# Splitting the second expert's up-projection in the last pair and moving its last part behind three output tiles

## The chip, the cores and the metric

One core of a Trainium2 chip runs the whole program. The metric is device time in microseconds of one execution. A core has TensorE (PE, with its weight loads shown as PEld), VectorE (DVE), ScalarE (ACT), GpSimd (POOL) and SyncE (SP); SP, ACT and POOL also issue DMAs. PSUM is where TensorE leaves its sums, and an engine must copy them out of it.

## The reference

Three stages follow each other. Attention of 2 batches, 8 heads and 576 positions with a learned distance bias gives x of 1152 tokens by 512. A dense layer with the gate h·sigmoid(h) and 2048 inner columns follows. Then comes a mixture of 8 experts, of which each token takes its best two:

```
for e in range(E):
    for k in range(2):
        mask = top2[:, k] == e
        h = np.maximum(x[mask] @ w1[e], 0.0)
        out[mask] += top2_w[mask, k, None] * (h @ w2[e])
```

w1[e] is 512 by 1024 and w2[e] 1024 by 512. Every token's row of the output is a sum over two experts.

## The kernel before

Products are made in two 16-bit halves (high and low), three matmuls to each: high·high, high·low, low·high. The experts are worked in four pairs, g = 0 to 3, by `experts(g)` (line 967). Each expert has 320 slots (`CAP`), and a token routed to it holds one. The gathered, transposed token rows of a pair lie in one tile `xg` of 640 columns: columns 0 to 319 are slots 0 to 319 of the first expert; of the second, columns 320 to 383 are slots 256 to 319, columns 384 to 511 slots 128 to 255, and columns 512 to 639 slots 0 to 127.

`up(k, c0, n)` (line 971) projects n columns from c0 of expert k up. It has eight groups, one for each 128 inner columns. A group is 12 matmuls (lines 979 to 981) into a PSUM tile `ph`, of which there are three; ACT takes the ReLU's high half out of it (line 985) and DVE the low half (line 986), into a tile `ht` of that expert and group.

`down(k, c0, col)` (line 989) makes an output tile for 128 slots: 24 matmuls of 512 columns (lines 995 to 997) over the eight `ht` into a PSUM tile `po`, of which there are two. `down_last()` (line 1001) makes the shared output tile: slots 256 to 319 of both experts, 64 rows each, in 48 matmuls with 64 weight columns (line 1010). `emit_out` (line 961) scales `po` on ACT into one of four SBUF tiles `ot` (line 964), and POOL adds the rows to the output in HBM with an indirect, accumulating DMA (line 958), here called a scatter. The shared tile has two scatters of 64 rows, the others have one of 128. All scatters add to the same output tensor, and each waits on POOL until the one before it has landed.

Each engine executes its own instructions in order. The order is made when the program is built: in general the order in which the code is written, but where a simulated timeline finds an instruction waiting, a later one that is ready may be put ahead. The last pair runs alone (line 1048); conversions and gathers of the earlier pairs are interleaved with the experts' work, but none are left here. After it comes a block for overfull experts (line 1053), which is not entered with these inputs, and the end of the program.

Of the kernel before, what the change touches and what calls it, by code (L numbers as in the profile page):

```python
# [23 lines left out]
CAP = 320  # L24
# [84 lines left out]
def body(ctx, tc, nc, A):  # L109
# [37 lines left out]
    def gen(name="gen"):  # L147
        return ps.tile([128, 512], F32, name=name, tag="gen", bufs=3)
# [484 lines left out]
    def chain(*gs):  # L633
        for g in gs:
            yield from g
# [325 lines left out]
    def emit_out(g, po, p0, n, col, icol):  # L961
        idx, ws = IDX[g]
        ot = m2o.tile([128, DM], F32, name="ot", tag="ot", bufs=4)
        SC.activation(ot[:n], po[p0:p0 + n, :DM], AF.Copy, scale=ws[p0:p0 + n, col:col + 1])  # L964
        scatter(idx[:n, 1, icol:icol + 1], ot[:n])

    def experts(g):
        xg = XG[g]
        hts = {}

        def up(k, c0, n):

            a_h, a_l = EW[2 * g + k, 0]
            for f in range(8):
                ph = gen("ph")[:, :n]
                for j in range(4):
                    cs = slice(1024 * j + 128 * f, 1024 * j + 128 * f + 128)
                    xh, xl = xg[:, j, c0:c0 + n], xg[:, 4 + j, c0:c0 + n]
                    mm(ph, a_h[:, cs], xh, start=(j == 0), stop=False)  # L979
                    mm(ph, a_h[:, cs], xl, start=False, stop=False)  # L980
                    mm(ph, a_l[:, cs], xh, start=False, stop=(j == 3))  # L981
                if (k, f) not in hts:
                    hts[k, f] = m2.tile([128, 2, CAP], F16, name="ht", tag="ht", bufs=20)
                ht = hts[k, f][:, :, c0 - CAP * k:c0 - CAP * k + n]
                SC.activation(ht[:, 0], ph, AF.Relu)  # L985
                V.scalar_tensor_tensor(ht[:, 1], ph, 0.0, ht[:, 0], op0=OP.max, op1=OP.subtract)  # L986
                yield

        def down(k, c0, col):
            b_h, b_l = EW[2 * g + k, 1]  # L990
            po = ps.tile([128, S], F32, name="po", tag="pq", bufs=2)
            for f in range(8):
                cs = slice(512 * f, 512 * f + 512)
                lh, ll = hts[k, f][:, 0, c0:c0 + 128], hts[k, f][:, 1, c0:c0 + 128]
                mm(po[:, :DM], lh, b_h[:, cs], start=(f == 0), stop=False)  # L995
                mm(po[:, :DM], lh, b_l[:, cs], start=False, stop=False)  # L996
                mm(po[:, :DM], ll, b_h[:, cs], start=False, stop=(f == 7))  # L997
            emit_out(g, po, 0, 128, col, col)
            yield

        def down_last():
            po = ps.tile([128, S], F32, name="po", tag="pq", bufs=2)
            for f in range(8):
                for x in range(3):
                    for kk in range(2):
                        bh, bl = EW[2 * g + kk, 1]
                        cs = slice(512 * f, 512 * f + 512)
                        c0 = 256 if kk == 0 else 0
                        lt = hts[kk, f][:, 1 if x == 2 else 0, c0:c0 + 64]
                        mm(po[64 * kk:64 * kk + 64, :DM], lt, (bl if x == 1 else bh)[:, cs],  # L1010
                           start=(f == 0 and x == 0), stop=(f == 7 and x == 2))
            emit_out(g, po, 0, 64, 4, 4)
            emit_out(g, po, 64, 64, 4, 5)
            yield

        if g == 0:
            yield from chain(up(0, 0, 128), up(1, 512, 128), down(0, 0, 0), down(1, 192, 1), up(0, 128, 192), up(1, 320, 192))
        else:
            yield from chain(up(0, 0, CAP), up(1, CAP, CAP))
        yield from down_last()  # L1020
        if g > 0:
            yield from chain(down(0, 0, 0), down(1, 192, 1))
        yield from chain(down(0, 128, 2), down(1, 64, 3))

    first = experts(0)
    for _ in range(X0):
        next(first)
# [16 lines left out]
    for g in range(4):  # L1044
        if g < 3:
            run((first if g == 0 else experts(g), 21), (conv_pair(g + 1), 16), (gather_pair(g + 1), 2))
        else:
            run((experts(g), 1))
# [85 lines left out]
```

## Time and profile before

| what | us |
|---|---|
| median of 3 runs | 755.66 |
| lowest and highest | 752.59, 762.42 |
| profiled execution, its time | 758.37 |
| profiled execution, its span | 756.6 |

The profile is of one execution. Its span goes from the first to the last recorded instruction; 1.77 us of its time lie around that. Times in rows are from the span's start. A matmul's own duration in a row includes its way through the array, so what a stream of them costs is read from the distance between starts.

### The profile page before, as it was taken

The numbers are of one execution on the slowest core, as the hardware profiler recorded it, in microseconds if no ns is written. First come the engines' busy times: TensorE is split into PE (matmuls) and PEld (weight loads), VectorE is DVE, ScalarE is ACT, GpSimd is POOL, SyncE is SP. The second block draws the span as 40 slices with busy tenths as digits, with TensorE's granted clock in tenths as the row PEclk, the third lists the DMA queues.
The fourth block names the chain that finished last, engine by engine and source line by source line (L and its number), as shares of the span: only waits on it lengthen the run. The fifth ranks groups of instructions, "written<-read, shape, count | busy, mean of one in ns | idle before, by whom it ended". The sixth has DMA issues, their size and how long they took to land.

```text
span 756.6 us, 16562 instructions
## 1 busy us (share of the span) xinstructions
PE 606.9 (80%) x6371; PEld 402.6 (53%) x6371; DVE 502.3 (66%) x1093; ACT 377.9 (50%) x805; POOL 366.5 (48%) x366
## 2 busy tenths in 40 slices
PE   0565666578587878997999889979889899999992
PEld 0462344456344666565765664757665554655640
DVE  2999999999999699556952755656657642740200
ACT  2666467668644577345732644761355543541210
POOL 2686677687967687436761552303405114103022
PEclk9875557599788998998999999999999999999996
DMA  4547788778876699887996967764999959903123
GB/s 113 135 140 243 158 161 179 183 210 186 159 179 182 161 174 199 145 172 116 159 237 124 183 129 220 192 225 110 238 240 246 308 182 230 299 4 42 17 25 43
DMA packets 203143, 125.77 MB, mean 166 GB/s; under 512 B 153076, under 2 KB 175732, under 8 KB 203060
## 3 DMA queue, kind: packets, MB, share of 16 engines
q1 hardware_dynamic: 170868, 90.39, 52.2%
q10 hardware_dynamic: 27648, 24.32, 11.0%
q0 software_dynamic: 4544, 9.97, 7.1%
q8 instruction: 51, 0.84, 0.4%
q14 instruction: 32, 0.26, 0.1%
HBM read 74.83 MB, written 18.22 MB: 123 GB/s over the span
## 4 chain that ended last, share of the span: by engine, by line
PE 29%; DVE 29%; DMA 18%; issue 11%; ACT 4%; POOL 4%; SPq 3%; ACTq 1%; another core or an unknown queue 1%; DVEq 0%; POOLq 0%
DMA stg<-in_e 6%; DVE mk L337 4%; PE ph L979 3%; DVE z L431 3%; DMA pt<-pr 3%; PE ph L981 3%; DVE pr L442 3%; PE ph L980 3%; DVE tt L504 3%; DVE tt L505 3%; PE po L1010 3%; DVE tt L500 2%; PE po L996 2%; PE po L995 2%; PE po L997 2%
## 5 line engine op out<-in xcount | busy, mean ns | idle before, releaser
L117 POOL TENSOR_TENSOR pr<-z,pr 128x512 f16<-128x512 f32 x72 | 94.6, 1321 | 23.3 <-ACT pr L438 14.7
L553 PE MATMUL ph<-xT,wb 128*128 128x256 f16 (+1 forms) x320 | 84.9, 275 | 11.5 <-DVE th L558 7.1
L345 PE MATMUL pb<-rhs_h,mk 128*128 128x64 f16 (+1 forms) x720 | 66.4, 210 | 26.4 <-ACT ta L361 11.6
L337 DVE TENSOR_TENSOR mk<-io,tau 128x1024 f16<-128x1024 f16 (+1 forms) x90 | 85.8, 959 | 0.7 <-PE pb L346 0.7
L117 POOL TENSOR_TENSOR gt<-th,gt 128x256 f16<-128x256 f32 (+1 forms) x80 | 56.0, 704 | 60.6 <-ACT gt L562 58.1
L117 POOL TENSOR_TENSOR g<-ta 128x256 f32<-128x256 f32 (+1 forms) x72 | 63.6, 884 | 44.3 <-ACT ta L361 37.4
L554 PE MATMUL ph<-xT,wb 128*128 128x256 f16 (+1 forms) x320 | 84.8, 275 | 0.0
L555 PE MATMUL ph<-xT,wb 128*128 128x256 f16 (+1 forms) x320 | 84.8, 275 | 0.0
L958 POOL DMA_INDIRECT out<-ot,idx x18 | 27.6, 1536 | 114.5 <-ACT ot L964 52.5
L388 PE MATMUL pq<-km,qt 128*128 128x512 f16 (+2 forms) x160 | 51.7, 437 | 28.9 <-DVE st L431 28.4
L436 ACT ACTIVATE z<-z,st 128x576 f32<-128x576 f32 x72 | 55.3, 769 | 34.9 <-DVE st L435 34.4
L986 DVE SCALAR_TENSOR_TENSOR ht<-ph,ht 128x320 f16<-128x320 f32 (+2 forms) x80 | 32.8, 420 | 54.3 <-ACT ht L985 53.8
L345 PEld LDWEIGHTS <-mk 128*128 128x128 f16 (+1 forms) x720 | 57.8, 111 | 19.3 <-issue 7.7
L346 PEld LDWEIGHTS <-mk 128*128 128x128 f16 (+1 forms) x720 | 56.9, 112 | 20.1 <-issue 19.2
L346 PE MATMUL pb<-rhs_l,mk 128*128 128x64 f16 (+1 forms) x720 | 65.9, 209 | 0.0
L924 DVE SCALAR_TENSOR_TENSOR wb<-stg,wb 128x1024 f16<-128x1024 f32 (+1 forms) x48 | 48.3, 1042 | 23.6 <-ACT wb L923 20.2
L923 ACT ACTIVATE wb<-stg 128x1024 f16<-128x1024 f32 (+1 forms) x48 | 41.8, 908 | 33.5 <-DMA stg<-in_e 29.9
L576 PE MATMUL py<-wb,gt 128*128 128x512 f16 x144 | 56.0, 391 | 1.5 <-DVE st L431 1.3
L577 PE MATMUL py<-wb,gt 128*128 128x512 f16 x144 | 56.1, 389 | 1.1 <-POOL wb L511 1.1
L578 PE MATMUL py<-wb,gt 128*128 128x512 f16 x144 | 55.8, 388 | 0.0
L985 ACT ACTIVATE ht<-ph 128x320 f16<-128x320 f32 (+2 forms) x80 | 29.2, 378 | 50.0 <-PE ph L981 49.8
L511 POOL TENSOR_TENSOR wb<-tt,wb 128x512 f16<-128x512 f32 x32 | 43.7, 1366 | 17.3 <-ACT wb L510 17.1
(198 smaller groups left out, 1794.0 us busy)
## 6 DMA issues: line engine op xcount, KB each, us to landing
stg<-in_e SPq DMA_DIRECT2D x64, 512.0 KB
raw<-in_w_in ACTq DMA_DIRECT2D x16, 512.0 KB
raw<-in_w_out ACTq DMA_DIRECT2D x16, 512.0 KB
bt<-eb SPq DMA_DIRECT2D x24, 288.0 KB
eb<-g SPq DMA_DIRECT2D x12, 512.0 KB
yrows<-yh SPq DMA_DIRECT2D x9, 256.0 KB
out<-zero SPq DMA_DIRECT2D x3, 768.0 KB
bt<-eb SPq DMA_DIRECT2D x16, 144.0 KB
```

The source lines that it names most:

```text
L117: G.tensor_tensor(o, x, y, op=op)
L337: i = V.tensor_tensor(mk[:, :, :n], io16[:, None, i0:i0 + n].to_broadcast([128, 8, n]), tv, op=OP.is_gt)
L345: mm(pb[:n, :, t, :], m, rhs_h, start=True, stop=False)
L346: mm(pb[:n, :, t, :], m, rhs_l, start=False, stop=True)
L388: i = mm(pq[p0:p0 + n, :512].rearrange("p (m s) -> p m s", m=2), lt, KM[b][r0:r0 + nr, :, h].rearrange("p m x s -> p m (x s)"), start=star ...
L436: SC.activation(z, z, AF.Exp, bias=st[:, 2:3], scale=0.125, accum_out=sums[:, bi, h % 4:h % 4 + 1])
L553: mm(ph, hh[:, cs], xh, start=(j == 3), stop=False)
L554: mm(ph, hh[:, cs], xl, start=False, stop=False)
L555: mm(ph, hl[:, cs], xh, start=False, stop=(j == 0))
L576: mm(pys[i], gh, oh[:, cs], start=(f == 0), stop=False)
L577: mm(pys[i], gh, ol[:, cs], start=False, stop=False)
L578: mm(pys[i], gl, oh[:, cs], start=False, stop=(f == 15))
```

## The change

Only the order and split inside `experts(3)` change. Before, the last pair ran up(0, all 320), up(1, all 320), the shared output tile, then the four tiles down(0,0), down(1,192), down(0,128), down(1,64). Now the second expert's up-projection is split into 192 columns (320 to 511) and 128 columns (512 to 639), and the 128 stand behind down(0,0), down(0,128) and the shared tile; down(1,64) and down(1,192) end the list. The other pairs are as they were.

```diff
         if g == 0:
             yield from chain(up(0, 0, 128), up(1, 512, 128), down(0, 0, 0), down(1, 192, 1), up(0, 128, 192), up(1, 320, 192))
+        elif g == 3:
+
+            yield from chain(up(0, 0, CAP), up(1, CAP, 192), down(0, 0, 0), down(0, 128, 2), down_last(), up(1, 512, 128),
+                             down(1, 64, 3), down(1, 192, 1))
+            return
         else:
             yield from chain(up(0, 0, CAP), up(1, CAP, CAP))
         yield from down_last()
```

## Rows read from the trace of the kernel before

**Rows 1.** The page: the span, and TensorE's granted clock in 40 slices (tenths).
```profile
span 756.6 us, 16562 instructions
...
PEclk9875557599788998998999999999999999999996
```
**Rows 2.** Chain of waits, 720 us to the end: start us, us, what.
```profile
736.98 0.69 ACT ot L964
...
743.53 4.76 DMA out<-ot,idx
...
749.04 1.55 POOL out L958
```
**Rows 3.** Timeline of POOL, last pair: start, us, instruction, idle before and its releaser.
```profile
723.38 1.43 POOL L958 DMA_INDIRECT out<-ot,idx  x1 [20.26 <-ACT ot L964]
727.73 1.42 POOL L958 DMA_INDIRECT out<-ot,idx  x1 [2.93 <-ACT ot L964]
732.09 1.57 POOL L958 DMA_INDIRECT out<-ot,idx  x1 [2.93 <-DMA out<-ot,idx]
737.85 1.57 POOL L958 DMA_INDIRECT out<-ot,idx  x1 [4.19 <-ACT ot L964]
743.53 1.55 POOL L958 DMA_INDIRECT out<-ot,idx  x1 [4.12 <-ACT ot L964]
```
**Rows 4.** Timeline of ACT, last pair: the first and the last output tile's scaling.
```profile
722.42 1.39 ACT L964 ACTIVATE ot<-po,ws 64x512 f32<-64x512 f32 x2 [4.27 <-PE po L1010]
...
742.16 0.69 ACT L964 ACTIVATE ot<-po,ws 128x512 f32<-128x512 f32 x1 [4.49 <-PEq L1053]
```
**Rows 5.** Stretches: length, busy us (instructions) by engine, clock (1.00 full), DMA share, GB/s.
```profile
695.30:717.50 22.20, 22.20 (x156) 14.59 (x154) 5.41 (x11) 5.49 (x12) 3.13 (x2) 1.00 0.20 25
...
722.20:741.90 19.70, 19.70 (x93) 8.84 (x91) 0.00 (x0) 3.43 (x5) 5.99 (x4) 1.00 0.31 36
```
**Rows 6.** Timeline of PE, last pair: a run of 36, the shared tile, a run of 91.
```profile
695.33 0.30 PE L979 MATMUL ph<-xg,ew 128*128 128x320 f16 x1
...
706.63 0.30 PE L979 MATMUL ph<-xg,ew 128*128 128x320 f16 x1
...
711.38 0.30 PE L981 MATMUL ph<-xg,ew 128*128 128x320 f16 x1
...
717.60 4.72 PE L1010 MATMUL po<-wb,ht 128*64 128x512 f16 x42
722.26 0.39 PE L997 MATMUL po<-wb,ht 128*128 128x512 f16 x1
...
741.70 0.38 PE L997 MATMUL po<-wb,ht 128*128 128x512 f16 x1
```
**Rows 7.** Timeline of PE, first pair: runs of 36 with 128 and 192 columns.
```profile
514.78 0.22 PE L979 MATMUL ph<-xg,ew 128*128 128x128 f16 x1
...
516.73 0.22 PE L981 MATMUL ph<-xg,ew 128*128 128x128 f16 x1
...
533.47 0.25 PE L979 MATMUL ph<-xg,ew 128*128 128x192 f16 x1
...
536.36 0.25 PE L981 MATMUL ph<-xg,ew 128*128 128x192 f16 x1
```
**Rows 8.** Groups by form: count | busy us, mean ns | idle before and releasers.
```profile
L979 PEld LDWEIGHTS <-ew 128*128 128x128 f16 x192 | 19.4, 101 | 5.0 <-issue 1.9
...
L986 DVE SCALAR_TENSOR_TENSOR ht<-ph,ht 128x128 f16<-128x128 f32 x16 | 4.4, 286 | 0.6 <-ACT ht L985 0.2
L985 ACT ACTIVATE ht<-ph 128x128 f16<-128x128 f32 x16 | 4.2, 278 | 5.4 <-PE ph L981 5.3
```
**Rows 9.** Timeline of PE, first pair: a matmul that waited for PSUM.
```profile
507.93 0.22 PE L979 MATMUL ph<-xg,ew 128*128 128x128 f16 x1 [1.47 <-DVE ht L986]
```
**Rows 10.** Stretches of the first pair: around a pause of PE, and after it.
```profile
543.20:546.30 3.10, 1.52 (x18) 0.74 (x16) 1.61 (x3) 1.49 (x3) 0.22 (x1) 1.00 1.14 280
546.70:549.70 3.00, 3.00 (x22) 2.85 (x20) 0.83 (x1) 1.50 (x3) 0.00 (x0) 0.50 1.14 295
```

## The prediction

> **What bounds the kernel now.** I read the page first. The span is 756.6 us, and the last slices of the clock line stand at 9, so TensorE has its full clock, the 2.4 GHz level, where the last pair runs [rows 1]. Then I read the end of the chain of waits, because this change moves work only in the last 60 us. The reader should see that the chain leaves TensorE before the program ends: from the scaling of the last but one output tile at 736.98 it goes to a scatter, to its DMA, to the next scatter, and the last scatter starts at 749.04 [rows 2]. TensorE's last matmul starts at 741.70 [rows 6], and the last tile's scaling runs from 742.16 to 742.85 [rows 4]. That tile then waits until 749.04 for POOL, though a scatter can start 0.18 us after its scaling (736.98 + 0.69 = 737.67, scatter at 737.85) [rows 2, 3]. So about 749.04 - 743.03 = 6.0 us of the end is a queue of scatters and not computation.
>
> Why there is a queue is seen in POOL's timeline [rows 3]. Six scatters stand one behind another from 723.38 on. The two of the shared tile take 4.35 and 4.36 us from start to start (727.73 - 723.38, 732.09 - 727.73). A whole tile's takes 5.68 (743.53 - 737.85) or 5.51 (749.04 - 743.53) [rows 2, 3]; I take 5.6. TensorE makes a whole tile in 24 matmuls at 0.216 us (741.70 - 722.26 over 90 steps) [rows 6], 5.18 us. The scatters are slower than the tiles, and the first one starts only when both up-projections and the shared tile are through. Until then POOL has been idle for 20.26 us [rows 3]. TensorE itself has no gap: it is busy 22.20 of 22.20 us and 19.70 of 19.70 us in the two long stretches [rows 5].
>
> **The change, part by part.**
>
> *TensorE's work.* The eight groups of 12 matmuls with 320 columns become 96 with 192 and 96 with 128. Paces, each over 35 steps: 320 columns 4.75 us, 0.1357 each [rows 6]; 128 columns 1.95 us, 0.0557 each; 192 columns 2.89 us, 0.0826 each [rows 7]. The split costs 96 x (0.0826 + 0.0557 - 0.1357) = 0.25 us. Its 96 extra weight loads are in that pace already, since the rows of the first pair have a load for each matmul. The downs and the shared tile are the same work as before.
>
> The trace also shows what changing between kinds of matmul costs. From 695.33, where the last 12 groups of 320 begin, the bare sum is 144 x 0.1357 + 48 x 0.111 (4.66 us for 42 [rows 6]) + 96 x 0.216 = 45.6 us, which would end at 740.9; it ended at 741.92, so 1.0 us went into such changes. The new order may keep that or lose it. I keep it, and carry 0 to -1.0 us as a bound. The new end of TensorE is 741.92 + 0.25 = 742.17.
>
> *Evictions.* Sixteen short ones replace eight: about 0.28 us each on ACT and DVE at 128 columns [rows 8]. ACT and DVE are busy 5.5 and 5.4 of 22.2 us there [rows 5], so TensorE's matmuls hide them. The one place without much cover is behind the shared tile: its two scalings hold ACT for 1.39 us [rows 4] while the 128-column groups, 0.67 us each, fill three PSUM tiles in 2.0 us. The first tile is free after some 0.16 + 1.39 + 0.28 + 0.29 = 2.1 us plus the handing over, a stall of a few tenths. The nearest row for a worse case is the first pair, where such a group waited 1.47 us for DVE [rows 9]. It can't gain, as nothing is taken away. Range 0 to +1.5; I take 0, because down(1,64) needs none of these columns and can fill the gap.
>
> *The scatters.* Number, size and DMAs stay at six; no other DMA is issued on any queue by the moved code. POOL has nothing but these scatters in the last pair, so the place in its queue is all that changes. From the end of a tile's last matmul to its scatter takes 0.24 + 0.69 + 0.18 = 1.11 us (741.92 to 742.16 [rows 4, 6], then as above). The new order on TensorE, from 695.33 without the 1.0 us of changes: four groups of the first expert 6.51 us, to 701.84; eight of 192 columns 7.93, to 709.77; down(0,0) to 714.95, scatter 716.1; down(0,128) to 720.1, scatter when POOL is free, 716.1 + 5.6 = 721.7; shared tile to 725.5, scatters 727.3 and 731.6, POOL free at 736.0. The 128 columns take 96 x 0.0557 = 5.35 us, to 730.8, and in that time the queue of scatters runs empty. With the changes between kinds (up to +1.0 on each time) and counted from the end: down(1,64) ends at 742.17 - 5.18 = 736.99, its scatter can start at 738.1 and POOL is free by 736.0 to 737.0. The last tile is ready at 742.17 + 1.11 = 743.28 but waits for that scatter, 738.1 + 5.6 = 743.7. This wait of 0.4 us is what comes next.
>
> *Sum.* The last scatter moves from 749.04 to 743.7, and the end stands 756.6 - 749.04 = 7.56 us behind it as before. The span becomes 751.3, a gain of 5.3 us. The profiled execution (758.37) would become 753.1; the median shown, 755.66, lies 2.7 us below it and becomes 750.4. If down(1,64) is finished earlier as a filler and the changes cost nothing, the gain is 5.3 + 0.4 + 1.0 = 6.7; with a full stall of 1.5 us it is 3.8.
>
> **Rivals.**
>
> *The order is not kept.* Ready instructions are put ahead of waiting ones: in the stretch to 717.5 there are 156 matmuls [rows 5], of which 144 are the 12 groups, and the shared tile's long run has 42 of its 48 [rows 6], so some were drawn forward. If the 128 columns were drawn ahead of the shared tile, its first scatter starts 5.35 us later, about 732.9 with the changes, and then 4.36 + 4.36 + 5.6 behind it the last one starts at 747.2: a gain of 1.8. Ahead of all tiles, the first scatter is at about 723.0, the last 5.6 + 5.6 + 4.36 + 4.36 + 5.6 = 25.5 later at 748.5: a gain of 0.5. Against it: the tiles are written first and their inputs are ready. Chance 12%.
>
> *Weight loads set the pace of the short matmuls.* A load takes 0.101 us by its row [rows 8], more than the 0.0557 and 0.0826 us of the matmuls. Paced so, they cost 96 x (0.0453 + 0.0184) = 6.1 us more: 0.8 us slower than before. Against it are the runs of 36, whose loads must have overlapped [rows 7]. Chance 2%. The Trainium skill ("TensorE: Matmul & The Clock Gate", section "Back-to-back issue gap") says that in a stream of pairs of load and matmul one with 128 columns takes about 81 ns. By it, as an estimate, the short stage costs 2.4 us more and the gain is 2.9; the trace disagrees, with 55.7 ns in the same matmuls.
>
> *A pause sets the clock back: slower than before.* Its place is the start of the 128-column groups, behind the shared tile's scalings. In the first pair TensorE stood still for half of a stretch of 3.1 us and ran the next 3.0 us at 0.50, the 1.2 GHz level [rows 10]. That price is 1.5 us. It decides only when the clock stays down for more than 10.6 us, half of which is the gain of 5.3. From there to the end are 5.35 + 10.36 = 15.7 us, so the worst is 15.7 - 5.3 = 10.4 us slower, 766. Against it: 22.20 of 22.20 us busy [rows 5] and only a few tenths of a stall expected. Chance 4%.
>
> **The numbers.** My forecast has 76%, the rivals 12, 2 and 4%, and 6% is for what I have not seen in the rest of the order. Time 750.4 us. Low end: the 1.0 us of changes, the 0.4 us of queue and the executions' own spread (752.59 against 755.66, 3.1 us) lead to 746. High end: no gain at all is 755.7, and with some of the spread 756.5. I leave the slow rival outside. A measurement of this kernel tells about 2%, 15 us, from no change. Nothing here gains 15 us, since the whole queue is 6.0; the slow rival reaches 10. So within 2% has 96%, faster 1%, slower 3%.
>
> **What would show it.** In the new trace the first scatter of the last pair starts near 716 and not 723; POOL is idle before the last but one; the last scatter starts near 743.7, less than 1 us after its tile is scaled; the end is 7.5 us later. The 128-column groups run at 0.056 us a matmul at full clock, and TensorE ends within 1 us of 742. I am wrong if the six scatters still stand without a gap, if TensorE has a hole of more than 1 us behind the shared tile, or if the trace before 695 has moved.

## The result and the profile after

The median went from 756.94 us to 749.38 us (21 runs each). The ratio is 0.9911, with a 95% interval of 0.9888 to 0.9935: 6.7 us less, between 4.9 and 8.5. It leaves out one execution of each kernel that was more than 1.5% slower than its fastest, so it isn't quite the difference of the medians, 7.6 us. The forecast had been 5.3 us less and a time of 750.4.

The spans of the two profiled executions, 756.6 and 747.5, differ by more than that. The instructions up to the last pair are the same in both kernels, and still the changed one reached the same matmul 2.56 us earlier (692.77 against 695.33 [rows 6]). Executions of one kernel differ by such amounts: a second profile of the changed kernel (below) came there at 698.52. So I compare the **tail**: from the first matmul of 320 columns behind the third pair's last output tile to the end of the span. It was 756.6 - 695.33 = 61.27 us and is 747.5 - 692.77 = 54.73, a gain of 6.5 us that agrees with the ratio.

POOL in the last pair of the changed kernel, with start, duration, instruction, and the idle time before it with what ended it:

```profile
713.61 1.56 POOL L958 DMA_INDIRECT out<-ot,idx  x1 [13.25 <-ACT ot L964]
719.19 1.56 POOL L958 DMA_INDIRECT out<-ot,idx  x1 [4.01 <-ACT ot L964]
724.60 1.43 POOL L958 DMA_INDIRECT out<-ot,idx  x1 [3.86 <-ACT ot L964]
728.91 1.42 POOL L958 DMA_INDIRECT out<-ot,idx  x1 [2.88 <-DMA out<-ot,idx]
733.39 1.57 POOL L958 DMA_INDIRECT out<-ot,idx  x1 [3.06 <-ACT ot L964]
739.91 1.57 POOL L958 DMA_INDIRECT out<-ot,idx  x1 [4.95 <-ACT ot L964]
```

The first scatter starts 20.8 us into the tail (713.61 - 692.77) and not 28.0 (723.38 - 695.33 [rows 3]), and the last 47.1 us and not 53.7 (749.04 - 695.33 [rows 2]). The end stands 7.59 us behind the last one (747.5 - 739.91), as it did before (7.56).

The releaser named in the brackets misleads here. The chain of waits tells more:

```profile
728.20 0.49 issue
...
728.91 3.56 DMA out<-ot,idx
...
732.51 0.65 issue
...
733.39 4.76 DMA out<-ot,idx
...
738.20 1.48 issue
...
739.91 1.57 POOL out L958
```

The second, third and fourth scatter start 0.75 to 0.78 us after their neighbour has landed, as the scatters of the queue before do (0.75 to 0.77), so they still stand in a queue, though the brackets name ACT at two of them. In that time the chain shows 0.49 us of issue. Ahead of the fifth scatter it shows 0.65, so POOL waits only 0.16 us for the tile; ahead of the last it shows 1.48, so POOL was ready 1.0 us before it. Only the first, the fifth and the last scatter start with their tile, 0.27 to 0.28 us after it has been scaled. What has gone from the end is not the queue but its last wait.

ACT at the end of the changed kernel:

```profile
712.64 0.69 ACT L964 ACTIVATE ot<-po,ws 128x512 f32<-128x512 f32 x1 [1.01 <-PE po L997]
...
723.13 1.39 ACT L964 ACTIVATE ot<-po,ws 64x512 f32<-64x512 f32 x2 [4.62 <-PE po L1010]
724.54 0.45 ACT L985 ACTIVATE ht<-ph 128x128 f16<-128x128 f32 x2
...
732.43 0.69 ACT L964 ACTIVATE ot<-po,ws 128x512 f32<-128x512 f32 x1 [1.07 <-PE po L997]
733.91 0.28 ACT L985 ACTIVATE ht<-ph 128x128 f16<-128x128 f32 x1 [0.80 <-PE ph L981]
734.59 0.28 ACT L985 ACTIVATE ht<-ph 128x128 f16<-128x128 f32 x1 [0.39 <-PE ph L981]
738.95 0.69 ACT L964 ACTIVATE ot<-po,ws 128x512 f32<-128x512 f32 x1 [4.09 <-PEq L1058]
```

The last tile is scaled at 739.64 and its scatter starts 0.27 us later; before, the last tile was scaled at 742.85 [rows 4] and waited 6.2 us. The last but one tile is scaled from 732.43 on, ahead of the last two evictions of the 128 columns. It was made between their groups, as TensorE's timeline shows:

```profile
717.67 5.37 PE L1010 MATMUL po<-wb,ht 128*64 128x512 f16 x48
722.97 0.23 PE L979 MATMUL ph<-xg,ew 128*128 128x128 f16 x1
...
724.94 0.22 PE L981 MATMUL ph<-xg,ew 128*128 128x128 f16 x1
724.99 0.38 PE L995 MATMUL po<-wb,ht 128*128 128x512 f16 x1
...
728.66 0.38 PE L997 MATMUL po<-wb,ht 128*128 128x512 f16 x1
728.88 0.22 PE L979 MATMUL ph<-xg,ew 128*128 128x128 f16 x1
...
730.83 0.22 PE L981 MATMUL ph<-xg,ew 128*128 128x128 f16 x1
730.89 0.38 PE L995 MATMUL po<-wb,ht 128*128 128x512 f16 x1
...
738.49 0.38 PE L997 MATMUL po<-wb,ht 128*128 128x512 f16 x1
```

The second run of 36 matmuls with 128 columns takes 1.95 us from its first start to its last, 0.0557 each. That is the pace of [rows 7]. TensorE has neither a hole nor a lower clock. These are stretches of the changed kernel's tail: length, busy time (instructions) of TensorE, its weight loads, VectorE, ACT and POOL, then the granted clock, the share of the DMA engines and GB/s:

```profile
692.77:711.10 18.33, 18.33 (x163) 14.38 (x162) 4.47 (x11) 4.75 (x12) 3.13 (x2) 1.00 0.23 30
711.10:717.50 6.40, 6.40 (x32) 2.84 (x30) 0.36 (x1) 1.02 (x2) 1.56 (x1) 1.00 0.30 34
717.50:722.95 5.45, 5.45 (x50) 2.63 (x48) 0.00 (x0) 0.69 (x1) 1.56 (x1) 1.00 0.37 49
722.95:738.70 15.75, 15.75 (x146) 9.98 (x144) 2.24 (x8) 4.16 (x11) 4.42 (x3) 1.00 0.27 34
```

### The profile page after: what moved, and what is told of

Read it like the earlier page. It is cut to its first block, busy times and chain, and to the rows that moved or that the text cites. A ratio compares the mean times of both kernels' runs of the same rounds, so it can differ in the third digit from the quotient of the medians.

```text
span 747.5 us, 16769 instructions
## 1 busy us (share of the span) xinstructions
PE 599.8 (80%) x6467; PEld 403.2 (54%) x6467; DVE 502.4 (67%) x1101; ACT 379.1 (51%) x813; POOL 367.1 (49%) x366
## 4 chain that ended last, share of the span: by engine, by line
PE 31%; DVE 28%; DMA 19%; issue 10%; ACT 5%; POOL 4%; SPq 2%; ACTq 1%; DVEq 0%; POOLq 0%
DMA stg<-in_e 6%; DVE mk L337 4%; DVE z L431 3%; PE ph L979 3%; DMA pt<-pr 3%; PE ph L981 3%; DVE pr L442 3%; PE ph L980 3%; DVE tt L504 3%; PE po L1010 2%; DVE tt L505 2%; DVE tt L500 2%; PE po L997 2%; PE po L996 2%; PE po L995 2%
## 5 line engine op out<-in xcount | busy, mean ns | idle before, releaser
L345 PE MATMUL pb<-rhs_h,mk 128*128 128x64 f16 (+1 forms) x720 | 64.7, 208 | 26.0 <-ACT ta L361 12.0
L337 DVE TENSOR_TENSOR mk<-io,tau 128x1024 f16<-128x1024 f16 (+1 forms) x90 | 82.5, 923 | 0.7 <-PE pb L346 0.7
L388 PE MATMUL pq<-km,qt 128*128 128x512 f16 (+2 forms) x160 | 49.6, 423 | 29.4 <-DVE st L431 29.0
L436 ACT ACTIVATE z<-z,st 128x576 f32<-128x576 f32 x72 | 55.3, 769 | 35.0 <-DVE st L435 34.6
L345 PEld LDWEIGHTS <-mk 128*128 128x128 f16 (+1 forms) x720 | 56.3, 110 | 19.3 <-DVE mk L337 8.2
L346 PEld LDWEIGHTS <-mk 128*128 128x128 f16 (+1 forms) x720 | 55.5, 110 | 19.5 <-issue 18.9
L346 PE MATMUL pb<-rhs_l,mk 128*128 128x64 f16 (+1 forms) x720 | 64.1, 207 | 0.0
L985 ACT ACTIVATE ht<-ph 128x320 f16<-128x320 f32 (+2 forms) x88 | 30.8, 359 | 57.5 <-PE ph L981 56.8
L576 PE MATMUL py<-wb,gt 128*128 128x512 f16 x144 | 55.3, 386 | 2.1 <-DVE st L431 1.9
L577 PE MATMUL py<-wb,gt 128*128 128x512 f16 x144 | 55.5, 385 | 1.6 <-POOL wb L511 1.6
L578 PE MATMUL py<-wb,gt 128*128 128x512 f16 x144 | 55.4, 384 | 0.0
L979 PE MATMUL ph<-xg,ew 128*128 128x128 f16 (+2 forms) x224 | 51.7, 249 | 2.0 <-DVE ht L986 2.0
```

Of the source, the lines that this page charges most:

```text
L337: i = V.tensor_tensor(mk[:, :, :n], io16[:, None, i0:i0 + n].to_broadcast([128, 8, n]), tv, op=OP.is_gt)
L345: mm(pb[:n, :, t, :], m, rhs_h, start=True, stop=False)
L346: mm(pb[:n, :, t, :], m, rhs_l, start=False, stop=True)
L436: SC.activation(z, z, AF.Exp, bias=st[:, 2:3], scale=0.125, accum_out=sums[:, bi, h % 4:h % 4 + 1])
L576: mm(pys[i], gh, oh[:, cs], start=(f == 0), stop=False)
L577: mm(pys[i], gh, ol[:, cs], start=False, stop=False)
```

## The experiments

Theory: each scatter waits for its neighbour to land; the queue of six behind a late first one cost the kernel before 6.0 us at its end, and the change lets it run empty before the last tile. Rivals: the finer pieces make TensorE faster; an early first scatter alone is enough; POOL's own work is the queue. All tails are counted as above. The tails are from one profile each, the ratios are to the kernel before. Each code cut is against the changed kernel unless the text says "in the kernel before"; `...` marks lines left out.

**The split without the move.**

```diff
-            yield from chain(up(0, 0, CAP), up(1, CAP, 192), down(0, 0, 0), down(0, 128, 2), down_last(), up(1, 512, 128),
-                             down(1, 64, 3), down(1, 192, 1))
+            yield from chain(up(0, 0, CAP), up(1, CAP, 192), up(1, 512, 128), down_last(), down(0, 0, 0), down(1, 192, 1),
+                             down(0, 128, 2), down(1, 64, 3))
```

> The last pair's second up-projection is split into 192 and 128 columns but not moved; the output tiles keep the old order. Tail means from the first matmul of 320 columns behind the third pair's last output tile to the end of the span: 61.3 us before, 54.7 us changed. Theory (the queue of six scatters behind a late first one sets the end): the first scatter stays late, about 28.8 us into the tail, and 4.36 + 4.36 + 3 x 5.6 later the last one starts; tail 61.3 to 61.9, time within 0.3% of before. Rival (the finer pieces let TensorE work more densely, and that is the gain): tail 57 or less, most of the gain of 6.5.

Ratio 1.0007 (0.9976 to 1.0038), tail 63.2. The queue stands without a gap:

```profile
724.06 1.43 POOL L958 DMA_INDIRECT out<-ot,idx  x1 [22.58 <-ACT ot L964]
728.47 1.42 POOL L958 DMA_INDIRECT out<-ot,idx  x1 [2.99 <-DMA out<-ot,idx]
732.77 1.57 POOL L958 DMA_INDIRECT out<-ot,idx  x1 [2.87 <-DMA out<-ot,idx]
738.41 1.57 POOL L958 DMA_INDIRECT out<-ot,idx  x1 [4.07 <-DMA out<-ot,idx]
744.07 1.55 POOL L958 DMA_INDIRECT out<-ot,idx  x1 [4.09 <-DMA out<-ot,idx]
749.63 1.55 POOL L958 DMA_INDIRECT out<-ot,idx  x1 [4.01 <-DMA out<-ot,idx]
```

The split alone gains nothing, so the rival of a faster TensorE falls. The tail is 1.3 us over my upper figure, because the first scatter comes 30.0 us into the tail (724.06 - 694.03) and not 28.8. In this program's order the shared tile is cut into six runs of 1 to 15 matmuls between the others, and TensorE ends 47.3 us into the tail against 46.6 before. That is 0.4 us more than the 0.25 us of the split. Eleven matmuls of the output tiles, and not five as before, were also drawn ahead of the shared tile's end, 6 x 0.216 = 1.3 us, which delay the first scatter.

**The move without the split.**

```diff
-            yield from chain(up(0, 0, CAP), up(1, CAP, 192), down(0, 0, 0), down(0, 128, 2), down_last(), up(1, 512, 128),
-                             down(1, 64, 3), down(1, 192, 1))
+            yield from chain(up(0, 0, CAP), down(0, 0, 0), down(0, 128, 2), up(1, CAP, CAP), down_last(), down(1, 64, 3),
+                             down(1, 192, 1))
```

> No split: the second expert's whole up-projection of 320 columns stands behind the first expert's two output tiles, and the shared tile and the second expert's two tiles follow. Theory (the scatters still to come when TensorE reaches the last tiles set the end): two scatters are out of the way early, but the shared tile ends only 10.4 us before TensorE does, so its two scatters and those of the last two tiles queue: last scatter at 36.7 + 4.36 + 4.36 + 5.6 = 51.0, tail about 58.5, a gain of 2.8 of the 6.5. Rival (starting the scatters early is enough, the split adds nothing): tail 54.5, the whole gain.

Ratio 0.9956 (0.9916 to 0.9996), tail 58.9, last scatter at 51.4 against the 51.0 worked out.

```profile
700.25 1.56 POOL L958 DMA_INDIRECT out<-ot,idx  x1 [5.95 <-ACT ot L964]
705.87 1.56 POOL L958 DMA_INDIRECT out<-ot,idx  x1 [4.06 <-ACT ht L985]
723.57 1.43 POOL L958 DMA_INDIRECT out<-ot,idx  x1 [16.13 <-ACT ot L964]
727.93 1.42 POOL L958 DMA_INDIRECT out<-ot,idx  x1 [2.94 <-DMA out<-ot,idx]
732.26 1.57 POOL L958 DMA_INDIRECT out<-ot,idx  x1 [2.91 <-DMA out<-ot,idx]
737.92 1.57 POOL L958 DMA_INDIRECT out<-ot,idx  x1 [4.08 <-DMA out<-ot,idx]
```

The first scatter is 7 us earlier than in the changed kernel (13.8 against 20.8 us into the tail), and yet most of the gain is missing. POOL is idle for 16.13 us in the middle, and four scatters queue at the end. What counts is how many are left when TensorE comes to its last tiles.

**The 128 columns ahead of the shared tile.**

```diff
-            yield from chain(up(0, 0, CAP), up(1, CAP, 192), down(0, 0, 0), down(0, 128, 2), down_last(), up(1, 512, 128),
+            yield from chain(up(0, 0, CAP), up(1, CAP, 192), down(0, 0, 0), down(0, 128, 2), up(1, 512, 128), down_last(),
...
```

> As changed, but the 128 columns stand ahead of the shared tile instead of behind it. TensorE has the same matmuls in nearly the same order. Theory: the shared tile's two scatters and those of the last two tiles queue again: tail about 58.6, a gain of 2.7 of the 6.5. Rival (the place of the 128 columns among the tiles does not matter, only that the first expert's tiles come early): tail 54.7.

Ratio 0.9998 (0.9962 to 1.0035), tail 59.0, with the last scatter at 51.5 us and TensorE's end at 46.4. The last scatter waits for its neighbour again:

```profile
742.12 1.57 POOL L958 DMA_INDIRECT out<-ot,idx  x1 [4.08 <-DMA out<-ot,idx]
```

By the tail 2.3 of the 6.5 us are gained. The timed runs don't resolve that 0.3%; their interval holds it. Against the changed kernel, one exchange of neighbours in the order costs 4.3 us of tail, while TensorE itself ends only 0.5 us later.

**Scatters that don't wait for their neighbour**, in the kernel before.

```diff
...
-        scatter(idx[:n, 1, icol:icol + 1], ot[:n])
+        spare = dap(EB[1], 0, [[DM, NT], [1, DM]])
+        scatter(idx[:n, 1, icol:icol + 1], ot[:n], spare if g == 3 and icol in (4, 0, 2) else None)
```

> The kernel before, but the last pair's scatters go in turn to the output and to a spare tensor of the same size, so that each waits for the one two places before it and not for its neighbour (three tiles' rows are then missing from the output). Theory (the wait for the landing of the neighbour is the queue): every scatter starts when its tile is ready, the last one at 47.7 us into the tail; tail 55.3, a gain of 6.0 without any change to TensorE's order. Rival (POOL's or the DMA engines' own work on a scatter is the queue, and a second target does not help): tail 61.3.

The lines left out hand `spare` on to the DMA as its target. Ratio 0.9932 (0.9893 to 0.9972), tail 55.2, where 55.3 was worked out.

```profile
717.69 1.43 POOL L958 DMA_INDIRECT eb<-ot,idx  x1 [20.77 <-ACT ot L964]
719.42 1.42 POOL L958 DMA_INDIRECT out<-ot,idx  x1 [0.30 <-issue]
721.97 1.57 POOL L958 DMA_INDIRECT eb<-ot,idx  x1 [1.12 <-ACT ot L964]
727.08 1.57 POOL L958 DMA_INDIRECT out<-ot,idx  x1 [3.54 <-ACT ot L964]
732.26 1.55 POOL L958 DMA_INDIRECT eb<-ot,idx  x1 [3.61 <-ACT ot L964]
737.44 1.55 POOL L958 DMA_INDIRECT out<-ot,idx  x1 [3.63 <-ACT ot L964]
```

TensorE's order is that of before. The second scatter follows the first after 1.73 us instead of 4.35, and the last four come at TensorE's pace, 5.1 to 5.2 us apart. So the queue is the wait for the landing and not POOL's work. This also shows what the queue was worth: 6.0 us of tail.

**Four scatters left out**, once in the kernel before and once in the changed one.

```diff
-        scatter(idx[:n, 1, icol:icol + 1], ot[:n])
+        if g < 3 or icol in (1, 3):
+            scatter(idx[:n, 1, icol:icol + 1], ot[:n])
```

> The kernel before without the last pair's first, second, third and fifth scatter (the shared tile's two and the first expert's two; those rows are missing from the output). Theory (the queue costs the kernel before 6.0 us at its end): the last scatter starts as soon as its tile is scaled, 47.7 us into the tail; tail 55.3. Rival (the end does not hang on the scatters before): tail 61.3.

> The changed kernel without the last pair's first four scatters (the first expert's two and the shared tile's two; those rows are missing from the output). Theory (in the changed kernel the queue of scatters has run empty by the end and TensorE sets it): tail 54.7 as with all six. Rival (scatters still delay the last one): a shorter tail, 54.3 or less.

The last scatter of each, first in the kernel before and then in the changed one:

```profile
743.42 1.56 POOL L958 DMA_INDIRECT out<-ot,idx  x1 [8.81 <-ACT ot L964]
```
```profile
744.26 1.56 POOL L958 DMA_INDIRECT out<-ot,idx  x1 [4.96 <-ACT ot L964]
```

Before: tail 55.1, last scatter 47.8 us into it and not 53.7. Changed: tail 54.4, last scatter at 47.1 us as with all six; the remaining 0.3 us lie behind it (7.3 against 7.6 us to the end). In the changed kernel the other scatters no longer delay the last one.

**The last but one tile held back** behind the 128 columns, profiled twice.

```diff
+                    LAST["up", g, k, c0] = mm(ph, a_l[:, cs], xh, start=False, stop=(j == 3))
...
-                mm(po[:, :DM], lh, b_h[:, cs], start=(f == 0), stop=False)
+                i = mm(po[:, :DM], lh, b_h[:, cs], start=(f == 0), stop=False)
+                if g == 3 and (k, c0, f) == (1, 64, 0):
+                    follow(i, ("up", 3, 1, 512))
```

> The changed kernel, but the second expert's output tile for slots 128 to 255 is held behind the last matmul of the 128 columns, so that it can't be drawn between their groups. Theory (the filling makes that tile ready earlier and so takes away the last wait of one scatter for the next, and covers a pause of TensorE behind the shared tile): a pause of some tenths, and the last scatter 5.6 us behind the one before, which starts 4.1 us before TensorE ends; tail 55.2 to 55.8. Rival (the filling does nothing): tail 54.7.

> The kernel with the tile for slots 128 to 255 held back, once more. In the first look its tail was 56.1, of which some 0.9 us was a last but one scatter that took 5.80 us to land. Theory (that landing was an accident, the wait of the last scatter is not): last scatter 5.5 to 5.7 us behind the one before, tail 55.1 to 55.3. Rival (held back, the scatter always lands late): tail 56 again.

Tails 56.1 and 55.7. TensorE ends 0.2 us later than in the changed kernel (46.14 against 45.94 us). In both the last tile waits again for the scatter before it, which starts at 42.2 us and not 40.6. That wait is the 0.4 us of the prediction and more, because the scatter before took longer to land. The chain of waits of the second profile:

```profile
729.66 5.37 DMA out<-ot,idx
...
735.78 1.57 POOL out L958
```

It landed after 5.80 us in the first profile and 5.37 in this one, against 4.76 in the changed kernel. I had called the first an accident, and that fell: 55.7 is nearer to 56 than to 55.3. Why it lands later is not shown, but the traces hold a candidate: in both, a packet of 16 KB of the queue that the page lists as `q8 instruction` begins while the scatter's own packets run, 3.71 and 2.98 us after its start. Such a packet takes 0.89 and 1.12 us here, and the last of the scatter's packets run behind it, until 5.35 and 5.01 us. In the changed kernel they end at 4.41 us, and that queue's packet begins only at 4.66.

**The last tile scaled by two engines.**

```diff
+        if g == 3 and icol == 1:
+            SC.activation(ot[:n, :256], po[p0:p0 + n, :256], AF.Copy, scale=ws[p0:p0 + n, col:col + 1])
+            V.tensor_scalar(ot[:n, 256:], po[p0:p0 + n, 256:DM], ws[p0:p0 + n, col:col + 1], None, op0=OP.mult)
...
```

> The changed kernel with the very last output tile scaled by ACT and VectorE together, 256 columns each, instead of 0.69 us on ACT alone. Theory (the end is TensorE's last matmul plus a fixed chain of scaling and one scatter): 0.2 to 0.3 us less, tail 54.4 to 54.5. Rival (the last scatter waits for the one before it): tail 54.7.

Tail 55.0. The edit failed at what it meant to do, since the halves ran one after the other. This is the timeline of the experiment's end:

```profile
746.50 0.47 ACT L965 ACTIVATE ot<-po,ws 128x256 f32<-128x256 f32 x1 [4.09 <-PEq L1062]
747.00 0.48 DVE L966 TENSOR_SCALAR ot<-po,ws 128x256 f32<-128x256 f32 x1 [4.27 <-ACT ot L965]
747.76 1.57 POOL L958 DMA_INDIRECT out<-ot,idx  x1 [5.06 <-DVE ot L966]
```

The scaling takes 0.98 us instead of 0.69, and the tail is 0.25 us longer. That is in line with an end that follows TensorE's last tile, and both expected figures are missed.

**The order in pairs 1, 2 and 3.** In pairs 1 and 2 the late columns meet weights of a later pair, because the weight tiles are reused in the written order. The amount of work is the same, but what these columns add to the output is not what the reference adds.

```diff
-        elif g == 3:
+        elif g > 0:
```

> The new order in pairs 1, 2 and 3 and not in the last alone. Theory (a queue of scatters costs only where no work follows it): no more than the change itself, time 0.99 of before, with 2 x 0.25 us more for TensorE; tail 54.7. Rival (the queue also holds up the pairs in the middle): 0.98 of before or less.

Ratio 0.9931 (0.9886 to 0.9977), the same as the change within the intervals, and no trace of 0.98. Where work follows, the queue costs nothing that these intervals, some 3 us to either side, can tell. The expected tail can't be read as such, because matmuls of the third and the last pair are mixed further here. Counted from TensorE's end the program ends 10.4 us later (753.2 - 742.83), against 8.8 in the changed kernel (747.5 - 738.71): the six scatters stand in a queue to the last, since two land late, one of 64 rows after 4.79 us and one of 128 after 5.98. So this end is 1.6 us longer than the change's.

**A second profile of the changed kernel.**

> The changed kernel once more, for a second profile of its end. Theory: the instructions up to the last pair are those of before, so that only the tail tells of the change; tail 54.4 to 54.8 whatever the whole span is. Rival (the gain of 6.5 in the tail was luck of one execution): a tail nearer to 61.3.

Span 753.2, tail 54.7, last scatter at 47.1 us, TensorE's end at 45.9. The tail repeats within 0.1 us while the rest of the span moves by 5.7.

## Why the prediction was right, point by point

- **The bound.** That a queue of scatters and not computation set the end, by 6.0 us, is shown from two sides: without the neighbour's wait the kernel before gains 6.0 us of tail, without four scatters 6.2. The 0.18 us from scaling to scatter were read where the neighbour's landing held the scatter too; with POOL free it is 0.27.
- **The order and the queue.** The first four scatters were worked out, without the cost of changes, for 20.8, 26.4, 32.0 and 36.3 us into the tail; they came at 20.8, 26.4, 31.8 and 36.1. In the 128 columns the queue runs empty by only 0.16 us ahead of the fifth scatter, where 1.1 to 2.1 had been forecast, since that tile came earlier; ahead of the last it is empty for 1.0 us, where a wait of 0.4 had been forecast.
- **The split's cost.** The paces of [rows 7] hold, and the weight loads don't set them; that rival is out.
- **The sum** was too small by 1.2 us: 6.5 us of tail where 5.3 stood. Two terms were mis-sized by 0.9 and 0.4 us, and both had been named as its bounds; the 0.27 instead of 0.18 us takes 0.1 back. The 1.0 us that changes between kinds of matmul cost [rows 6] was kept, but only some 0.1 is left: TensorE ends 45.94 us into the tail, and the bare sum is 45.6 + 0.25. The shared tile now goes in one run of 48, where 6 of its matmuls had been drawn ahead singly or in small runs. And the 0.4 us wait of the last scatter is gone, because down(1,64) is drawn between the groups of 128 columns. I had named that filling as cover for a stall and put its effect on the last scatter into the upper bound only. That the time of 750.4 came within 1.0 us is in part luck: it was worked from the median of three executions, 755.66, and all 21 give 756.94, from which a gain of 5.3 leads to 751.6.
- **The pause behind the shared tile** didn't come: ACT's 1.39 us there are covered by three groups and 18 matmuls of down(1,64). The clock stayed at full in the stretches of the tail, so the slow rival had nothing to start from. Of the clock before, the very last slice stands at 6 and not at 9 [rows 1]; most of it lies behind TensorE's last matmul, and it is the 1.00 of [rows 5] that carries the reading.
- **The rival of the order** was half right. Instructions are drawn forward, but from the tiles behind and not the 128 columns from behind the tiles. Its price was about right: with the 128 columns ahead of the shared tile the tail gains 2.3 us, and 1.8 was worked out. For the 128 columns ahead of all tiles the terms give a first scatter at 716.1 + 5.35 + 1.0 = 722.4 and not 723.0, so a gain of 1.1 and not 0.5; that order was not run.
- **A sign of being wrong came by the letter:** the trace before 695 moved, by 2.56 us. The instructions there are the same, and a second execution of the changed kernel lies 5.7 us further on, so the sign tells nothing about the change.

## What to carry to other kernels

When accumulating scatters to one tensor wait for one another, compare their distance (here 5.5 to 5.7 us for 128 rows) with that of the tiles that feed them (5.2 us); if it is larger, the end of the program is the first scatter plus the whole queue, and tiles should be finished early enough that the queue has run out when the last tile is ready. Delaying matmul work that only the last tile needs does that at almost no cost, but its place decides: one position further forward lost two thirds of the gain. Judge such a change by its own stretch of the profile, since the part of the program before it, the same in all of them, took from 686.5 us (whole move) to 698.5 (second profile of the change) in these profiles, and the whole gain is 6.5.

## What was not expected of the hardware

A scatter of 128 rows of 512 took 4.7 to 5.1 us from start to landing in the last pair of all these kernels, except for five that took 5.37 to 6.01: the two held back, and one each with the whole move, with two targets and with the order in three pairs. Into each of the five a 16 KB packet of `q8 instruction` fell, 2.98 to 4.29 us after the scatter's start. Such a packet is not enough: one at 3.94 us, also with two targets, left a scatter at 4.74 us. That it delays the scatter is likely, but no run tests it. One of 64 rows still needs 4.35 us from start to start [rows 3], more than three quarters of a whole one's time for half the rows. And cutting the shared tile's matmuls into small runs between full-width ones cost TensorE up to 1.4 us: with the split alone it ended 47.3 us into the tail, where the bare sum is 45.9. The starts of the matmuls put 0.2 to 0.3 us of it to each of the six runs.
